# Loading f once and turning the first batch's q and k in two parts, in a fused forgetting-attention and bilinear feed-forward kernel

## The chip, the core and the metric

The kernel runs on one core of one Trainium2 chip. The metric is the device time of one execution in microseconds. A core has a matrix engine (TensorE, PE in the profile), a vector engine (VectorE, DVE), a scalar engine with activation tables (ScalarE, ACT), a general engine (GpSimd, POOL), a sync engine that issues DMAs (SyncE, SP), and 16 DMA engines. Each engine runs its own instructions in the order in which they were written, and waits on semaphores for what other engines produce. PEld in the profile is the loading of weights into TensorE, which overlaps its matmuls.

## The reference

Two stages follow each other. The first is causal attention with a forgetting gate over 8 batches, 8 heads, 576 positions and a head size of 64:

```python
scores = scale * np.matmul(q, k.transpose(0, 1, 3, 2))
log_f = np.log(np.clip(f, 0.0001, 1.0))
cum = np.cumsum(log_f, axis=-1)
decay = cum[:, :, :, None] - cum[:, :, None, :]
scores = np.where(causal, -1000000000.0, scores + decay)
attn = exp(scores - max) / sum
out  = np.matmul(attn, v)
```

The second takes the attention's output as 4608 tokens of 512 numbers and computes `(x @ w_a) * (x @ w_b) @ w_out` with an inner size of 1536. All inputs and the output are float32.

## The kernel before

**Attention.** The work is tiled by t, a pair of heads of one batch (32 tiles), and by u, two tiles that share one set of score matmuls (16 groups of four heads). Within a tile the rows fall into blocks i = 0 to 4 of 128 positions (the last has 64), and only blocks at or below the diagonal are computed. Four score groups g cover the rows: g 0 holds blocks 1 and 0, g 1 block 2, g 2 block 3, g 3 block 4 (`qk_group`, lines 383 to 440).

q and k come in as float32, 128 partitions of 4 heads times 32 slots (`load_qk`, line 280). They are cast to float16 (`cast_qk`, through the helper `cast`, lines 137, 139 and 141) and turned by VectorE's 32x32 transpose (`transpose_qk`, line 294), so that the head's 64 dimensions lie on four row groups of 32 partitions. A score matmul therefore uses 32 rows, and four heads run side by side on the four row groups.

**The decay.** Only the part that depends on the key position matters for a softmax over keys. The cumulated logarithm of f is added to the scores of the first two batches by TensorE: a matmul of a one-hot column (`pick`) with the tile `crow` (line 390, `mm(y, pick, crow)`). `crow` holds, in each of the four row groups of 32 partitions, 16 rows with the high part of the cumulated values in float16 and 16 rows with the low part, so that one matmul adds both. These 16 rows are the heads of batches 0 and 1. For later batches the cumulated values are stored to DRAM (`cum_store`, line 226) and loaded again, spread over all partitions (`load_spread`, line 452), and are added by VectorE.

In the kernel before, f is loaded twice into one tile of 128 partitions: partitions 0 to 63 receive the first 16 rows four times, partitions 64 to 127 all 64 rows (`f_load`, line 194). VectorE clips (line 205), ScalarE takes the logarithm (line 208), VectorE cumulates by a scan (line 212), in two ranges of columns, 0 to 256 and 256 to 576. VectorE then makes `crow` for partitions 0 to 63 from the high part (line 216) and a selector `lsel` (line 219), and a copy puts the same rows into partitions 64 to 127 (line 223).

**Softmax.** For the first two batches (the direct ones) VectorE takes the maximum straight from the scores in PSUM (line 484), ScalarE the exponential with the sum (lines 537, 543), VectorE the reciprocal (lines 550, 552), and GpSimd normalises (line 560). The first batch's probabilities are transposed by TensorE (`pe_tr`, line 584) and copied out of PSUM, those of later batches by DMA (line 576). Products with v (lines 604, 606, 616, 629) are copied into `xT`, which is what the feed-forward stage reads.

**Feed-forward.** For each block of 256 to 512 tokens and each of 12 slices of the inner size, four matmuls give `psa` and four `psb` (line 877). ScalarE or VectorE copies `psa` to float16, VectorE multiplies it with `psb` (line 888), and matmuls with `wout` follow (line 897). The weights come in by GpSimd's DMAs, which also cast them (line 357). The tiles for the second half of the first batch's q and k lie in the memory of `wout` until `wout` is loaded.

**Fillers.** 40 groups of four matmuls on the identity matrix (line 174), whose results nobody uses, stand in TensorE's order at places where it has nothing else to do.

**The order.** All operations are written down first, 2342 of them, each with the engines that may run it. Two tables then fix everything: `ORDER` lists operation numbers in the sequence in which they are issued, and `CHOICE` gives one letter for each operation that has several engines to choose from (A for ScalarE, D for VectorE, P for GpSimd, S for SyncE). No planner runs in the kernel. The feed-forward blocks of early batches are interleaved on TensorE with the attention of later ones.

In the order before, the first operations of SyncE's queue are: f (16 rows four times), k and q of heads 0 to 3, k and q of heads 4 to 7, the first part of v, k and q of the second batch's first half, the last part of v, the store of the cumulated values. ScalarE issues the other load of f. GpSimd's sequence is: paddings (memsets, lines 167 and 169), identity matrix, casts of k and q of heads 0 to 3 in two parts each, the copy of `crow`, a weight load, half of a q cast, a weight load, the other half, a weight load, a cast of v, then normalisations.

Of the kernel before, what the change touches and what calls it, by code (L numbers as in the profile page):

```python
# [37 lines left out]
def kernel(  # L38
# [46 lines left out]
    lsel = fixed("lsel", [128, 1], FP32)  # L85
# [10 lines left out]
    chigh = wout16.rearrange("p n k -> p (n k)")[:, 4608:4608 + S]  # L96
# [60 lines left out]
    def picks(_):  # L157
        nc.vector.tensor_reduce(out=lsel, in_=ident.rearrange("p (a x r) -> p x a r", x=2, r=16)[:, 1],
                                axis=AXXY, op=ADD, negate=True)
# [3 lines left out]
        nc.vector.tensor_scalar(out=neg, in0=eye, scalar1=NEGBIG, scalar2=1.0, op0=MUL, op1=MUL)  # L163

# [20 lines left out]
    def f_tiles():  # L185
        x = [s_pool.tile([128, 1024], FP32, tag="S", name=n) for n in ("cum_f", "cum_l")]
        cw["f"], cw["l"] = x[0][:, 0:S], x[1][:, 0:S]
        cw["1"] = x[0][:, S:].bitcast(FP16)[:, 0:S]

    def f_load(e, m):  # L190
        rows = f.rearrange("b h s -> (b h) s")
        if m == 0:
            rows = bass.AP(rows.tensor, 0, [[0, 4], [S, 16], [1, S]])
        ENG[e].dma_start(out=cw["f"][HP[m]], in_=rows)
# [8 lines left out]
    def clip(lo, hi):  # L203
        x = cw["f"][:, lo:hi]
        nc.vector.tensor_scalar(out=x, in0=x, scalar1=1e-4, scalar2=1.0, op0=MAX, op1=MIN)
# [4 lines left out]
    def scan(lo, hi):  # L210
        x = cw["f"]
        nc.vector.tensor_tensor_scan(out=x[:, lo:hi], data0=cw["1"][:, lo:hi], data1=cw["l"][:, lo:hi],
                                     initial=x[:, lo - 1:lo] if lo else 0.0, op0=MUL, op1=SUB)

    def high_part(lo, hi):
        nc.vector.tensor_copy(out=chigh[HP[0], lo:hi], in_=cw["f"][HP[0], lo:hi])

    def rows_part(lo, hi):
        nc.vector.scalar_tensor_tensor(out=crow[HP[0], lo:hi], in0=chigh[HP[0], lo:hi], scalar=lsel[HP[0]],
                                       in1=cw["f"][HP[0], lo:hi], op0=MUL, op1=ADD)  # L220

    def rows_again(e, lo, hi):
        ENG[e].tensor_copy(out=crow[HP[1], lo:hi], in_=crow[HP[0], lo:hi])

    def cum_store(_):
        nc.sync.dma_start(out=cum_d, in_=cw["f"][HP[1]])

    f_tiles()
    o_f = [op("AS", "ldf", lambda e, m=m: f_load(e, m), size=m) for m in range(2)]
    s_users = [take(o_f[0], "S") for _ in range(2)]  # L230
    o_f[1].after.append(o_f[0])
    o0 = op("D", "ones", f_ones, [])
    o0.after.append(o_f[0])
# [895 lines left out]
```

## Time and profile before

| What | Value |
|---|---|
| Median of the runs shown | 403.06 us (403.03 to 404.61) |
| The profiled execution | 402.69 us |
| Its span | 400.9 us |
| Busy share of PE, DVE, POOL, ACT | 95%, 79%, 66%, 63% |
| Granted TensorE clock, mean | 0.985 of full speed |
| First score matmul starts | 13.34 us |
| First feed-forward matmul starts | 33.89 us |

The span goes from the first to the last record of the program on the core; the time of the execution holds some 1.8 us more around it. A row of the timeline gives the start, the length, the engine and line of one instruction or of a run of like ones (x2, x52), and in brackets the idle time of the engine just before and what ended it. Where a row has no bracket, its engine did not wait. SPq, ACTq and POOLq are the queues of an engine that issue a DMA: the length there is the issuing, not the transfer. The time to landing is given by rows of their own.

### The profile page before, as it was taken

The page shows a single profiled execution, that of the slowest core. Times are in us where ns is not written, and L with a number is a line of the kernel's source. Part 1 is how long each engine was busy: PE and PEld are TensorE (multiplying, and loading weights), DVE is VectorE, ACT ScalarE, POOL GpSimd, SP SyncE. Part 2 cuts the span into 40 slices and gives each one's busy share as a digit, 9 for nine tenths or more (in the row PEclk, how much of TensorE's full clock was granted, in tenths as well). Part 3 has the DMA queues.
Part 4 walks back from the last instruction along what each step waited for, and adds up shares of the span by engine and source line. Part 5 has one row for each costly group of instructions (what it writes and reads, how often), then busy time and mean ns, then how long its engine had stood idle before and what let it go on. Part 6 is the DMA issues. An engine that isn't in the chain of part 4 may idle for free.

```text
span 400.9 us, 10798 instructions
## 1 busy us (share of the span) xinstructions
PE 378.9 (95%) x3856; PEld 209.3 (52%) x3856; DVE 315.5 (79%) x958; ACT 250.6 (63%) x756; POOL 262.8 (66%) x438
## 2 busy tenths in 40 slices
PE   5679799989999999999999999999999999999996
PEld 5557575765846544444545454544454444444553
DVE  5879997979998988989899789899959893373450
ACT  2678895768768777758785777675868673310111
POOL 4988899787967796979696948697858753000000
PEclk9869999999999999999999999999999999999999
DMA  7999999999999999999899998999997827101102
GB/s 245 261 217 224 253 284 224 233 209 225 208 281 224 267 199 305 202 310 191 270 217 286 238 301 168 242 242 243 255 199 192 151 68 177 54 0 53 55 2 78
DMA packets 149466, 80.71 MB, mean 201 GB/s; under 512 B 130660, under 2 KB 133476, under 8 KB 149412
## 3 DMA queue, kind: packets, MB, share of 16 engines
q1 hardware_dynamic: 145492, 75.02, 79.1%
q0 software_dynamic: 3696, 4.72, 7.0%
q8 instruction: 30, 0.49, 0.5%
q10 hardware_dynamic: 224, 0.28, 0.2%
q14 instruction: 24, 0.20, 0.1%
HBM read 52.20 MB, written 9.58 MB: 154 GB/s over the span
## 4 chain that ended last, share of the span: by engine, by line
PE 69%; DMA 8%; DVE 8%; POOL 5%; ACT 4%; issue 4%; SPq 0%; POOLq 0%; ACTq 0%; DVEq 0%
PE psb L877 20%; PE psa L877 20%; PE pso L897 16%; PE sc L390 7%; DVE st L484 3%; PE pv L604 2%; DMA PTB<-PB 2%; POOL PA L560 2%; DMA spread<-cum_d 2%; DMA k<-in_k_dram 2%; PE idle L174 1%; DVE ht L888 1%; DVE S L508 1%; DMA out_dram<-osb 1%; DMA xT<-PA 1%
## 5 line engine op out<-in xcount | busy, mean ns | idle before, releaser
L877 PE MATMUL psb<-xT,wb 128*128 128x512 f16 (+2 forms) x528 | 115.2, 341 | 2.4 <-DVE a L141 1.3
L877 PE MATMUL psa<-xT,wa 128*128 128x512 f16 (+2 forms) x528 | 115.2, 341 | 0.5 <-ACT osb L137 0.2
L508 DVE CUSTOM_DVE_ANT_0 S<-sc,spread 128x128 f32<-128x128 f32 (+3 forms) x192 | 104.3, 567 | 7.8 <-PE sc L390 6.7
L560 POOL TENSOR_SCALAR PA<-PA,st 128x128 f16<-128x128 f16 (+2 forms) x180 | 84.4, 482 | 33.8 <-DVE st L552 19.8
L897 PE MATMUL pso<-wout,ht 128*128 128x512 f16 (+1 forms) x444 | 98.4, 374 | 0.0
L888 DVE TENSOR_TENSOR ht<-psb,a 128x512 f16<-128x512 f32 (+2 forms) x132 | 76.7, 588 | 14.1 <-PE psb L877 10.1
L543 ACT ACTIVATE PA<-S,st 128x256 f16<-128x256 f32 (+2 forms) x144 | 71.9, 501 | 22.9 <-DVE st L508 21.4
L877 PEld LDWEIGHTS <-wb 128*128 128x128 f16 x528 | 49.8, 98 | 45.7 <-issue 6.8
L877 PEld LDWEIGHTS <-wa 128*128 128x128 f16 x528 | 50.4, 98 | 42.7 <-issue 2.0
L560 POOL TENSOR_SCALAR PB<-PB,st 128x512 f16<-128x512 f16 (+1 forms) x90 | 62.8, 712 | 10.6 <-DVE st L552 5.9
L897 PEld LDWEIGHTS <-ht 128*128 128x128 f16 x444 | 41.8, 98 | 48.1 <-issue 2.8
L137 ACT CAST a<-psa 128x512 f16<-128x512 f32 (+2 forms) x85 | 42.7, 511 | 34.8 <-PE psa L877 33.4
L390 PE MATMUL sc<-kT,qT 32*128 32x128 f16 (+5 forms) x960 | 41.3, 272 | 6.8 <-DVE qT L294 4.6
L543 ACT ACTIVATE PB<-S,st 128x512 f16<-128x512 f32 x48 | 34.3, 716 | 8.1 <-DVE st L508 7.4
L484 DVE TENSOR_REDUCE st<-sc 128x1 f32<-128x576 f32 (+8 forms) x48 | 31.4, 693 | 6.8 <-PE sc L390 5.2
L141 DVE CAST a<-psa 128x512 f16<-128x512 f32 (+2 forms) x47 | 26.2, 558 | 11.3 <-PE psa L877 10.8
L390 PEld LDWEIGHTS <-qT 32*128 32x128 f16 (+1 forms) x960 | 19.0, 96 | 28.8 <-issue 12.3
L552 DVE RECIPROCAL st<-st 128x2 f32<-128x2 f32 x128 | 18.6, 157 | 11.5 <-ACT PB L543 6.1
L537 ACT ACTIVATE PB<-S,st 128x576 f16<-128x576 f32 x24 | 18.6, 775 | 13.9 <-DVE st L508 5.0
L543 ACT ACTIVATION_READ_ACCUMULATOR PA<-S,st 128x1 f32 x144 | 27.2, 189 | 0.0
L137 ACT COPY osb<-pso 128x512 f32<-128x512 f32 (+1 forms) x26 | 14.4, 563 | 20.3 <-PE pso L897 18.6
L141 POOL CAST k<-k 128x1152 f16<-128x1152 f32 (+2 forms) x16 | 22.1, 1384 | 5.0 <-DMA k<-in_k_dram 5.0
(87 smaller groups left out, 449.8 us busy)
## 6 DMA issues: line engine op xcount, KB each, us to landing
spread<-cum_d SPq DMA_DIRECT2D x24, 576.0 KB, 5.9
out_dram<-osb SPq DMA_DIRECT2D x35, 256.0 KB, 4.0
k<-in_k_dram SPq DMA_DIRECT2D x15, 576.0 KB, 6.5
q<-in_q_dram SPq DMA_DIRECT2D x15, 576.0 KB, 6.9
v<-in_v_dram SPq DMA_DIRECT2D x32, 256.0 KB, 6.7
wout<-in_moe_w_out_dram POOLq DMA_DIRECT2D x3, 512.0 KB, 11.0
wa<-in_moe_w_a_dram POOLq DMA_DIRECT2D x1, 1024.0 KB, 13.9
v<-in_v_dram SPq DMA_DIRECT2D x8, 128.0 KB, 6.0
```

Of the source, the lines that this page charges most:

```text
L137: nc.scalar.copy(out=out_, in_=in_)
L141: ENG[e].tensor_copy(out=out_, in_=in_)
L390: nc.tensor.matmul(out=dst, lhsT=lhsT, rhs=rhs, start=start, stop=stop, skip_group_check=True)
L484: nc.vector.tensor_reduce(out=m if i == 4 else st[:, 2 * i:2 * i + 2][:, h:h + 1] if isinstance(x, list) else m, in_=y, axis=AXX, op=MAX, ...
L508: nc.vector.tensor_tensor_reduce(out=o, in0=x, in1=y, scale=-1.0, scalar=3e38, op0=ADD, op1=MIN, accum_out=m)
L537: nc.scalar.activation(out=p_blocks(t, 4), in_=T[("s" if direct else "z", t, 4)], func=EXP, bias=st[:, 8:9], scale=sign, accum_out=st[:, 1 ...
L543: nc.scalar.activation(out=p_blocks(t, i)[:, :, h, :], in_=x.rearrange("p (j k) -> p j k", k=128), func=EXP, scale=sign, bias=st[:, c:c + ...
L552: nc.vector.reciprocal(out=st[:, 20 + 2 * i:22 + 2 * i], in_=st[:, 10 + 2 * i:12 + 2 * i])
L560: ENG[e].tensor_scalar(out=p, in0=p, scalar1=st[:, c:c + 1], scalar2=1.0, op0=MUL, op1=MUL)
L877: nc.tensor.matmul(out=p[:, 0:n], lhsT=w16[:, db, 128 * fb:128 * fb + 128], rhs=xTflat[db][:, t0:t0 + n], start=(db == 0), stop=(db == 3))
L888: nc.vector.tensor_tensor(out=ht[:, 0:n], in0=T.pop(("psb", t0, fb))[:, 0:n], in1=T.pop(("a16", t0, fb))[:, 0:n], op=MUL)
L897: nc.tensor.matmul(out=o, lhsT=T[("ht", t0, fb)][:, 128 * tb:128 * tb + 128], rhs=wout16[:, fb, c], start=(fb == 0), stop=(fb == 11))
```

## The change

The program now has 2351 operations. Four things differ.

1. **f.** All 64 rows are loaded once, into partitions 0 to 63, by one DMA; clip, logarithm and scan work on 64 partitions. From the first 32 partitions a high part in float16 and a low part (the value less the high part) are put into a scratch tile `parts`. TensorE then spreads them: two accumulating matmuls with a matrix of zeros and ones, `sel`, put the high part into the first 16 and the low part into the second 16 rows of all four row groups, and one copy out of PSUM makes `crow`. `sel` is made on VectorE with a memset and two copies; `lsel` and the copy between partition halves go.
2. **q and k of the first batch** are loaded, cast and turned in two parts: tokens 0 to 255 and tokens 256 to 575. The first scores of a group (g 0, blocks 0 and 1) depend on the first parts alone; before, they depended on the whole. Casts were in two parts before, split at 5 of 9, and are now split at 4 of 9; a transpose now depends only on the cast of its part. Each part's load may be issued by SyncE or ScalarE.
3. **New numbers and a new order.** `ORDER` and `CHOICE` are replaced.
4. A small function `turns` names which parts TensorE transposes; they are the same ones as before.

```diff
-    chigh = wout16.rearrange("p n k -> p (n k)")[:, 4608:4608 + S]
+    sel = spare[2][0:32, 1536:1792].rearrange("p (e m) -> p e m", e=2)
+    parts = wout16.rearrange("p n k -> p (n k)")[0:32, 4608:4608 + 2 * S].rearrange("p (e s) -> p e s", e=2)
...
+        nc.vector.memset(sel, 0.0)
+        for e in range(2):
+            nc.vector.tensor_copy(out=sel[:, e].rearrange("p (g e r) -> p g e r", e=2, r=16)[:, :, e],
+                                  in_=eye[0:32, 0:16].unsqueeze(1).to_broadcast([32, 4, 16]))
...
-    def f_load(e, m):
-        rows = f.rearrange("b h s -> (b h) s")
-        if m == 0:
-            rows = bass.AP(rows.tensor, 0, [[0, 4], [S, 16], [1, S]])
-        ENG[e].dma_start(out=cw["f"][HP[m]], in_=rows)
+    def f_load(e):
+        ENG[e].dma_start(out=cw["f"], in_=f.rearrange("b h s -> (b h) s"))
...
-    def rows_part(lo, hi):
-        nc.vector.scalar_tensor_tensor(out=crow[HP[0], lo:hi], in0=chigh[HP[0], lo:hi], scalar=lsel[HP[0]],
-                                       in1=cw["f"][HP[0], lo:hi], op0=MUL, op1=ADD)
-
-    def rows_again(e, lo, hi):
-        ENG[e].tensor_copy(out=crow[HP[1], lo:hi], in_=crow[HP[0], lo:hi])
+    def high_part(e, lo, hi):
+        cast(e, parts[:, 0, lo:hi], cw["f"][0:32, lo:hi])
+
+    def low_part(e, lo, hi):
+        ENG[e].tensor_tensor(out=parts[:, 1, lo:hi], in0=cw["f"][0:32, lo:hi], in1=parts[:, 0, lo:hi], op=SUB)
+
+    def rows_mm(lo, hi):
+        c = T[("rows", lo)] = ps.tile([128, 512], FP32, tag="ff", bufs=RING["ff"], name="rows")
+        for e in range(2):
+            nc.tensor.matmul(out=c[:, 0:hi - lo], lhsT=sel[:, e], rhs=parts[:, e, lo:hi], start=e == 0, stop=e == 1)
+
+    def rows_ev(e, lo, hi):
+        cast(e, crow[:, lo:hi], T.pop(("rows", lo))[:, 0:hi - lo])
...
+    SPLIT = [(0, 4), (4, TW)]
...
+    def load_part(e, which, hh, m):
...
+        lo, hi = SPLIT[m]
+        src = src_of[which][0, 4 * hh:4 * hh + 4, 64 * lo:64 * hi, :].rearrange("h (s t) d -> h s (t d)", s=NSLOT)
+        ENG[e].dma_start(out=T[key][:, 128 * lo:128 * hi], in_=src)
...
-    def transpose_qk(b, which, hh):
+    def transpose_qk(b, which, hh, lo=0, hi=TW):
...
-                deps = [T_ops[(x, 0, u)] for x in "qk"] + [o_low, o_pick] + crow_ops[:1 if g == 0 else 2]
+                deps = [y for x in "qk" for y in T_ops[(x, 0, u)][:1 if g == 0 else 2]] + [o_low, o_pick] + crow_ops[:1 if g == 0 else 2]
```

The two tables are too long to show. Decoded, the new sequences begin as follows (q00 is the first part of q of heads 0 to 3, q01 its second part, q10 and q11 the parts of heads 4 to 7, and so for k):

| Engine | New sequence at the start |
|---|---|
| SP, loads | f, k00, q01, k01, q10, v blocks 0 and 1, k11, q of batch 1, store of the cumulated values, v of batch 1, k of batch 1 |
| ACT | load q00, logarithm's table, both logarithms, loads q11 and k10, cast q01, cast k01, `crow` first range out of PSUM, exponential's table, cast k10, three exponentials of the first tile, `crow` second range, exponentials |
| POOL | identity matrix, cast k00, cast q00, load of wa from column 512 on, load of wb up to column 512, casts q10 and q11, paddings, cast of v, twelve normalisations, load of wa up to column 512 |
| DVE | selectors, ones, masks, both clips, scan, high and low part of the first range, turn k00, scan of the second range, turn q00, q01, k01, maxima of the first tile, high and low part of the second range, a maximum of the second tile, turn k10 and q10, a maximum and two reciprocals, cast k11, maxima of the second pair |
| PE | 14 fillers, spreading of the first range, filler, scores g 0 of heads 0 to 3, 5 fillers, spreading of the second range, 5 fillers, scores g 0 of heads 4 to 7 |

After the first batch the new sequence on TensorE sets each score group behind nearly the same number of feed-forward matmuls as the old one.

185 lines of the change are left out of this document (97 added, 88 removed), and 133 rows, old and new, of the table ORDER.

## The prediction

> **What bounds the kernel now.** I read the windows first, then the timeline of the first 34 us, then the landing times of the DMAs issued there. The profiled execution took 402.69 us, 1.8 more than its span:
>
> ```profile
> span 400.9 us, 10798 instructions
> ```
>
> The columns of the next two fences are the stretch, its length, the busy time of PE, PEld, DVE, ACT, POOL (the second: PE and PEld of the filler matmuls of line 174 alone), the granted clock, the DMA share and GB/s.
>
> ```profile
> 0.00:4.00 4.00, 1.13 (x11) 1.14 (x12) 1.72 (x7) 1.49 (x2) 2.09 (x12) 1.00 0.39 78
> 4.00:8.00 4.00, 4.00 (x51) 4.00 (x49) 1.61 (x9) 0.78 (x2) 0.17 (x1) 1.00 1.00 327
> ...
> 0.00:34.00 34.00, 22.72 (x370) 19.55 (x370) 25.12 (x63) 20.23 (x65) 25.78 (x50) 0.85 0.98 237
> 34.00:57.00 23.00, 20.32 (x383) 15.98 (x382) 21.46 (x51) 19.84 (x56) 19.45 (x29) 1.00 1.09 249
> 80.00:320.00 240.00, 236.98 (x2292) 120.00 (x2293) 211.42 (x723) 173.64 (x534) 188.09 (x314) 1.00 1.03 235
> 320.00:380.00 60.00, 60.00 (x400) 28.94 (x397) 31.22 (x68) 17.73 (x42) 9.33 (x17) 1.00 0.25 68
> ```
>
> ```profile
> 0.00:34.00 34.00, 12.92 (x144) 11.67 (x144) 0.85 0.98 237
> ```
>
> From 80 us on PE is never without work: 3.0 us idle in 240, none in the 60 after that, where the other engines are mostly idle and PE drains feed-forward matmuls that have long been ready. So the end is set by the amount of PE work plus what PE loses early. Up to 34 us PE is busy 22.72 us, 12.92 of it fillers, so 9.8 us of real work in 34 us. A microsecond gained ahead of the first feed-forward matmul is a microsecond off the end, as long as nothing behind it slips. Read the other way: the chain there is worth 24 us, and the rest of the kernel has little to give.
>
> The timeline of that stretch (start, duration, engine, line, operation, and the idle time before with its releaser):
>
> ```profile
> 0.73 0.56 ACTq L194 DMA_DIRECT2D cum_f<-in_f_dram  x1
> 0.74 0.75 SPq L194 DMA_DIRECT2D cum_f<-in_f_dram  x1
> 1.19 0.99 POOL L169 MEMSET nv<- 64x512 f16 x2
> 1.55 0.54 SPq L280 DMA_DIRECT2D k<-in_k_dram  x1
> 4.11 3.85 SPq L264 DMA_DIRECT2D v<-in_v_dram  x2
> 6.78 0.53 DVE L205 TENSOR_SCALAR cum_f<-cum_f 128x256 f32<-128x256 f32 x2 [2.03 <-DMA cum_f<-in_f_dram]
> 7.11 0.78 ACT L208 ACTIVATE cum_l<-cum_f 128x256 f32<-128x256 f32 x2 [4.28 <-DVE cum_f L205]
> 7.83 2.52 POOL L141 CAST k<-k 128x640 f16<-128x640 f32 x2 [5.02 <-DMA k<-in_k_dram]
> 8.28 0.76 DVE L216 CAST wout<-cum_f 64x256 f16<-64x256 f32 x1
> 10.34 1.55 POOL L139 TENSOR_SCALAR q<-q 128x640 f16<-128x640 f32 x2
> 11.64 1.50 ACT L137 CAST k<-wout 128x640 f16<-128x640 f32 x2 [3.75 <-DVE kT L294]
> 12.09 1.19 DVE L294 STREAM_TRANSPOSE qT<-q 128x576 f32<-128x576 f32 x1
> 12.87 0.94 POOL L357 DMA_DIRECT2D wa<-in_moe_w_a_dram  x1 [0.16 <-issue]
> 13.16 1.28 ACT L201 ACT_TABLE_LOAD   x1
> 13.34 0.40 PE L390 MATMUL sc<-kT,qT 32*128 32x256 f16 x8 [4.64 <-DVE qT L294]
> 14.40 4.32 PE L174 MATMUL idle<-ident 128*128 128x128 f16 x52
> 14.51 1.29 DVE L484 TENSOR_REDUCE st<-sc 128x2 f32<-128x512 f32 x2
> 15.24 0.47 ACT L543 ACTIVATE PA<-sc,st 128x256 f16<-128x256 f32 x1 [0.58 <-DVE st L484]
> 17.00 1.05 POOL L141 CAST nv<-v 128x1024 f16<-128x1024 f32 x1
> 18.08 0.69 SPq L264 DMA_DIRECT2D v<-in_v_dram  x1
> 18.32 2.30 POOL L560 TENSOR_SCALAR PA<-PA,st 128x128 f16<-128x128 f16 x5 [0.27 <-DVE st L552]
> 18.65 0.50 PE L390 MATMUL sc<-kT,qT 32*128 32x256 f16 x8
> 20.36 0.47 ACT L543 ACTIVATE spread<-sc,st 128x256 f16<-128x256 f32 x1 [0.94 <-DVE st L484]
> 33.89 0.60 PE L877 MATMUL psa<-xT,wa 128*128 128x256 f16 x4
> ```
>
> The first scores start at 13.34 because q's transpose ends then, behind two whole casts on POOL, behind a k that is usable at 7.83. The cumulated f is no gate here. The second pair of head groups starts its scores at 18.65, the exponentials of that pair at 20.36, the first feed-forward matmul at 33.89.
>
> **The change, part by part.** Its order, decoded from operation numbers, puts each group of scores after the same amount of feed-forward work as before: never more than 1.9 us of matmuls apart (count of columns at the pace of this trace), equal for most groups after the third batch. So I take the middle and the tail at no change, with that as the bound, and work out the start alone.
>
> *Loads.* A part of k or q is 4/9 (262 KB) or 5/9 (328 KB) of 590 KB. The order of need is f (147 KB), q's first part on ACT's queue, k's first part, q's second, k's second on SP's. Delivered so far: 4 x 78 = 312 KB by 4 us, then 327 KB a microsecond. Whole k of before stands behind two f loads, 885 KB in all, which this pace passes at 5.75; its cast starts at 7.83, 2.1 later, and I take that offset for every part. First k part: 671 KB, 5.1, usable at 7.2. Second q part: 999 KB, 8.2. Second k part: 1327 KB, 9.2.
>
> ```profile
> cum_f<-in_f_dram ACTq DMA_DIRECT2D x1, 144.0 KB, 2.7
> wout<-in_q_dram SPq DMA_DIRECT2D x1, 576.0 KB, 9.0
> wa<-in_moe_w_a_dram POOLq DMA_DIRECT2D x1, 1024.0 KB, 13.9
> wa<-in_moe_w_a_dram POOLq DMA_DIRECT2D x1, 512.0 KB, 8.5
> wb<-in_moe_w_b_dram POOLq DMA_DIRECT2D x1, 512.0 KB, 9.7
> v<-in_v_dram SPq DMA_DIRECT2D x1, 128.0 KB, 11.4
> ```
>
> These rows give KB and us from issue to landing. *f* is now loaded once. It lands between 3.4 (issue 0.73 plus 2.7, as on ACT's queue) and 6.78 (as now). Even at 6.78, scan, high part, low part and the spreading matmuls follow within 3 us (the high part's cast was 0.76 at its worst), before 9.9, so this part by itself is worth nothing: it lies under the k and q loads. What it removes, half a DMA of descriptors and the copies between partition halves, hides there too.
>
> *Casts and transposes.* POOL casts the first parts: k 7.2 to 8.4 (half of 2.52, a little less for 512 columns), q to 9.2 (half of 1.55). DVE turns them, half of 1.19 each, to 9.8. ACT casts the second parts, 0.75 each: q 8.2 to 9.0, k 9.2 to 10.0, and only then evicts the spread f rows (not in this trace; the nearest row is the 0.47 of the exponential, which reads as many columns from PSUM; half and twice that are the bounds, I take 0.4). First scores: 10.4 against 13.34, 2.9 earlier. The two second-part transposes (0.66 each) end at 11.1 on DVE, the maxima start 1.2 after the scores as now: 11.6 against 14.51. ACT loads the exponential's table from 10.4 to 11.9 (1.28 and a warming call), casts the first part of the second k (0.73), and starts the exponentials at 12.6 against 15.24: 2.6 earlier.
>
> *POOL's queue.* The paddings (nv's 0.99 and four smaller memsets, 1.5 in all by the first row's start and the identity matrix behind them) move from ahead of the identity matrix to ahead of v's cast. The identity comes 1.5 sooner, which only starts fillers sooner. Behind the first q cast at 9.2 POOL has two weight issues (0.94 each), both casts of the second q (1.55) and the paddings: v's cast from 14.2 to 15.3, then twelve normalisations at 2.30/5, to 20.8. Before, the normalisations started at 18.32.
>
> *Second pair.* Behind the maxima of the first tile DVE has the f tail's high and low part and the next maxima (about 2.5 together), then two half transposes: 15.3, so its scores at 15.3 against 18.65. The ten fillers between the two groups of scores (40 matmuls at 4.32/52) take 3.3 from about 11.5, so they end about then too. DVE then casts the last k part (0.75, as on ACT) ahead of the maxima of the second pair; exponentials at 17.5 against 20.36: 2.8 earlier. That part, issued behind v at 8.0, lands 2.7 to 9.0 later, 10.7 to 17.0; DVE comes to it at about 16, so the late end would cost 1.0. I take it as landed by then, and keep the 1.0 for the range.
>
> *Sum.* The three gates move by 2.6 to 3.4, and I carry 2.8, less 0.2 for four spreading matmuls, two more casts and four more issues, to the first feed-forward matmul: about 31.3. 402.69 - 2.6 = 400.1 for a profiled execution; the median shown lies 0.37 above that execution, hence 400.4. The unknown costs: filling the selector and the low part's subtraction on DVE, each between nothing and the 0.76 of line 216. The first lies under the 2.03 that DVE waited for f, the subtraction for the first columns under the load of k, and both are taken at nothing; with that cover gone up to 1.5 would come onto the sum. The cast of the last k part on DVE, which was not there, is 0.75 and is on the path; it is counted.
>
> A rule on the first part of the second k, ACT's last load. Here ACT's f landed in 2.7 while SP's f, issued with it, held the clip until 6.78. The Trainium skill, "DMA: Bandwidth & Descriptors", section "Queues, rings and completion order", says that each DMA engine takes packets in turn from every queue that has work, so a short queue need not wait for a long one; the two f rows agree. By that rule this part lands early and the sum stays 400.4; by the rows of SP's queue alone it would be that of the first rival.
>
> **Rivals.** *Hidden anyway.* ACT's last k part is issued behind both logarithms (now ending 7.89) and two issues of 0.56, so by 9.0 at the latest. It lands 2.7 (ACT's empty queue) to 9.0 (fifth on SP's) later, 11.7 to 18. ACT's cast of it stands ahead of every exponential, so from a landing at 14.5 on nothing is left of the gain. The last k part on SP holds DVE's maxima in the same way from 18.5 on. For it: the queues are full from 4 us on. Against: ACT's queue has been the quick one. Price: the gain falls to 0 to 1; 402.6.
>
> *Slower: the weights.* POOL now issues 1.5 MB of weights right after the first q cast, from 9.2 instead of 12.87, and issues the 512 KB of wa that the first feed-forward matmul needs only behind twelve normalisations, which stand behind the cast of v. A v issued into the weights landed in 11.4. v's second DMA is issued by 7.96 and would land at 19.4, be cast by 20.4, the normalisations (2.30/5 each) end at 25.9, and wa land 10.7 later (mean of 8.5, 9.7 and 13.9) at 36.6, 2.7 after 33.89: 405.4, on the median 405.8. It decides once v lands after 16.7. Against: v is issued before the weights now, and its cast at 17.00 waited for no DMA. In the forecast v is in by 14.2, the normalisations end at 20.8, and wa, now last of the weights, lands in the 8.5 of its own row, at 29.3, 2.0 before it is needed.
>
> *More than that.* If earlier batch-1 inputs also close the 2.7 us of idle between 34 and 57, 400.4 - 2.7 = 397.7. Against: DVE is 93% busy there.
>
> **How the numbers follow.** Forecast 0.52 (its own range 399.0 to 401.8), hidden 0.24, slower 0.13, more 0.11. What a measurement can tell from 403.06 is about 0.5%, so 401.05 and 405.07 are the bounds: faster 0.59 (most of the forecast and all of "more"), same 0.28, slower 0.13. Range 397.9 to 404.8, which leaves out most of the slower case and the lower half of "more", 0.15 to 0.2 in all.
>
> **What would show it.** First scores near 10.4, with ACT's eviction of the f rows as the last thing they wait for; exponentials near 12.6 and 17.5; first psa near 31.3, the 80 to 320 stretch as busy as now. It is wrong if psa waits for the DMA of wa, if ACT or DVE idles for a k part after 13 us, or if PE idles more than 3.0 us between 80 and 320.

## The result, and the profile after

The changed kernel is slower. Its median is 425.89 us (425.33 to 428.38) against 403.65 us (403.03 to 404.61) of the kernel before on the same chip, a ratio of 1.056 (95% interval 1.051 to 1.061), some 22 us more. The forecast was 400.4, the upper end of the range 404.8. The profiled execution took 426.45 us.

The page of the changed kernel, its span and two of the rows of 40 slices (tenths of busy time; a slice is 10.6 us):

```profile
span 424.7 us, 10828 instructions
...
PE   5042789997899999999999999999999999999996
...
DMA  2937789989999999999999999999988927300102
```

TensorE is almost idle in the second slice and at two tenths in the fourth, and the DMA engines are at 0.2 and 0.3 in the first and the third (the weights, which GpSimd issues at 10.6 and 11.6, fill the second). The stretch from 4 to 10 us, in which the first q and k travel, after and then before (columns as in the prediction, the last two being DMA share and GB/s):

```profile
4.00:10.00 6.00, 3.03 (x39) 2.54 (x37) 1.95 (x6) 0.78 (x2) 0.72 (x2) 1.00 0.26 102
```

```profile
4.00:10.00 6.00, 4.70 (x60) 4.52 (x57) 3.42 (x11) 0.78 (x2) 2.17 (x2) 1.00 1.01 355
```

Loads were issued and waiting all the time, and yet the 16 DMA engines were busy for 0.26 of it, against 1.01 before, and moved 102 GB/s instead of 355. A quarter of the engines at work would look like this. The timeline of the changed kernel shows what waited for it:

```profile
4.06 0.52 DVE L204 TENSOR_SCALAR cum_f<-cum_f 64x256 f32<-64x256 f32 x2
4.43 21.83 SPq L269 DMA_DIRECT2D v<-in_v_dram  x2
9.28 0.71 POOL L141 CAST k<-k 128x512 f16<-128x512 f32 x1 [7.97 <-DMA k<-in_k_dram]
11.95 0.40 PE L412 MATMUL sc<-kT,qT 32*128 32x256 f16 x4 [4.92 <-DVE qT L308]
13.11 0.87 ACT L135 ACTIVATE q<-q 128x640 f16<-128x640 f32 x1 [7.96 <-DMA q<-in_q_dram]
19.91 0.86 ACT L137 CAST k<-k 128x640 f16<-128x640 f32 x1 [5.93 <-DMA k<-in_k_dram]
21.61 0.40 PE L412 MATMUL sc<-kT,qT 32*128 32x256 f16 x4 [9.26 <-DVE kT L308]
...
29.92 1.54 POOL L139 TENSOR_SCALAR q<-wout 128x512 f16<-128x512 f32 x2 [17.59 <-DMA wout<-in_q_dram]
...
54.87 0.60 PE L902 MATMUL psa<-xT,wa 128*128 128x256 f16 x4
```

f comes early (clip at 4.06 instead of 6.78), but the first k part is cast at 9.28, the second parts of q and k at 13.11 and 19.91, the second q at 29.92, and SyncE is held for 21.83 us in the issue of v. The first feed-forward matmul starts at 54.87 instead of 33.89, 21.0 us later; the end follows with 22. The eight parts together hold 2 x 2 x (256 + 320) KB = 2304 KB, 2.36 MB, which at 102 GB/s alone would take 23 us.

One sentence of "The change" does not hold on the chip: that the first scores of a group depend on the first parts alone. Only their first four matmuls, over the first half of the head size, do so (11.95, behind the first transpose of q). The others wait until 21.61 for the second transpose of k, which follows the cast at 19.91. So the second parts set the first scores here too. The second transpose writes columns of the same tile on both sides of those that these other matmuls read; that they wait for this reason fits the code, but no run tests it.

Three stretches of the changed kernel:

```profile
0.00:34.00 34.00, 11.31 (x144) 9.61 (x144) 10.71 (x31) 7.18 (x14) 6.62 (x18) 0.72 0.54 128
34.00:57.00 23.00, 14.73 (x234) 10.72 (x238) 15.89 (x41) 16.71 (x61) 16.23 (x28) 0.67 0.76 186
...
80.00:320.00 240.00, 233.72 (x2377) 122.45 (x2376) 207.62 (x693) 173.51 (x535) 188.80 (x310) 1.00 1.08 236
```

No engine is busy for more than a third of the first 34 us, and TensorE runs at a granted clock of 0.72 and 0.67 up to 57 us, where it had 0.85 and 1.00 before. From 80 us on the matmuls stand nearly as close as before (6.3 us idle in 240, against 3.0).

### The profile page after: what moved, and what is told of

Same layout as the page of the kernel before. It is cut to its first block, busy times and chain, and to the rows that moved or that the text cites. A ratio compares the mean times of both kernels' runs of the same rounds, so it can differ in the third digit from the quotient of the medians.

```text
span 424.7 us, 10828 instructions
## 1 busy us (share of the span) xinstructions
PE 381.6 (90%) x3860; PEld 209.8 (49%) x3860; DVE 313.1 (74%) x960; ACT 255.8 (60%) x764; POOL 258.7 (61%) x434
## 3 DMA queue, kind: packets, MB, share of 16 engines
HBM read 52.05 MB, written 9.58 MB: 145 GB/s over the span
## 4 chain that ended last, share of the span: by engine, by line
PE 64%; DMA 11%; POOL 7%; SPq 6%; DVE 5%; issue 3%; ACT 3%; POOLq 0%; ACTq 0%; DVEq 0%
PE pso L922 19%; PE psb L902 17%; PE psa L902 16%; PE sc L412 6%; SPq L269 5%; DMA wout<-in_k_dram 3%; POOL PB L582 3%; DMA spread<-cum_d 2%; DMA PTB<-PB 2%; POOL PA L582 2%; DVE st L506 2%; DMA xT<-PA 2%; PE pv L626 2%; DVE ht L913 1%; ACT spread L565 1%
## 5 line engine op out<-in xcount | busy, mean ns | idle before, releaser
L582 POOL TENSOR_SCALAR PA<-PA,st 128x256 f16<-128x256 f16 (+2 forms) x180 | 83.8, 480 | 38.2 <-DVE st L574 27.0
L913 DVE TENSOR_TENSOR ht<-psb,a 128x512 f16<-128x512 f32 (+2 forms) x132 | 76.3, 587 | 19.6 <-PE psb L902 16.1
L565 ACT ACTIVATE PA<-S,st 128x256 f16<-128x256 f32 (+2 forms) x144 | 72.0, 502 | 21.8 <-DVE st L530 19.6
L137 ACT CAST a<-psa 128x512 f16<-128x512 f32 (+2 forms) x92 | 46.7, 511 | 37.5 <-PE psa L902 29.5
L308 DVE STREAM_TRANSPOSE kT<-k 128x576 f32<-128x576 f32 (+2 forms) x18 | 19.7, 1097 | 18.0 <-ACT k L137 14.2
L137 ACT COPY osb<-pso 128x512 f32<-128x512 f32 (+1 forms) x26 | 14.5, 566 | 25.1 <-PE pso L922 23.5
L480 POOL TENSOR_SCALAR_AFFINE_SELECT spread<-spread 128x768 f32<-128x768 f32 x24 | 20.8, 868 | 13.2 <-DMA spread<-cum_d 13.2
L574 DVE RECIPROCAL st<-st 128x2 f32<-128x2 f32 x128 | 18.8, 157 | 12.6 <-ACT PA L565 8.4
L141 DVE CAST a<-psa 128x512 f16<-128x512 f32 (+2 forms) x40 | 22.6, 564 | 6.7 <-PE psa L902 6.3
L137 ACT CAST xT<-pv 128x512 f16<-128x512 f32 (+2 forms) x37 | 16.7, 456 | 17.8 <-PE pv L628 11.5
```

The source lines that it names most:

```text
L137: nc.scalar.copy(out=out_, in_=in_)
L141: ENG[e].tensor_copy(out=out_, in_=in_)
L480: nc.gpsimd.affine_select(out=c[:, :, 0:SM].rearrange("p h (j k) -> p h j k", k=128), in_=c[:, :, SM:2 * SM].rearrange("p h (j k) -> p h j ...
L565: nc.scalar.activation(out=p_blocks(t, i)[:, :, h, :], in_=x.rearrange("p (j k) -> p j k", k=128), func=EXP, scale=sign, bias=st[:, c:c + ...
L582: ENG[e].tensor_scalar(out=p, in0=p, scalar1=st[:, c:c + 1], scalar2=1.0, op0=MUL, op1=MUL)
L913: nc.vector.tensor_tensor(out=ht[:, 0:n], in0=T.pop(("psb", t0, fb))[:, 0:n], in1=T.pop(("a16", t0, fb))[:, 0:n], op=MUL)
```

## The experiments

All ratios are to the kernel before on the same chip, with the 95% interval; "us" beside them is the ratio's distance from 1 times that kernel's median there (404.5 to 405.4).

**contig16: parts that are contiguous.** This kernel reads other tokens than the change does. What differs between a whole load and a part is the shape of its source. The whole load's heads and slots merge into one dimension of 128; a part is a slice of each head, so its slowest dimension is the 4 heads.

```diff
-        src = src_of[which][0, 4 * hh:4 * hh + 4, 64 * lo:64 * hi, :].rearrange("h (s t) d -> h s (t d)", s=NSLOT)
+        x = src_of[which][0, 4 * hh:4 * hh + 4].rearrange("h s d -> (h s d)")
+        src = x[0:128 * 128 * (hi - lo)].rearrange("(p x) -> p x", p=128)
```

> The changed kernel, with the eight part loads reading one contiguous stretch of the same number of bytes instead of their tokens (so q and k of the first batch hold other tokens; the work on them is the same). Same number of DMAs, same bytes to each partition, same order. Theory A (a part load, whose source is four heads by 32 slots, moves on four of the 16 DMA engines; the changed kernel shows a DMA share of 0.26 at 102 GB/s from 4 to 10 us, 4/16 = 0.25): all part loads are usable by 13 us, DMA share near 1 from 4 us on, first feed-forward matmul near 31 us, time 397 to 404, as my prediction's steps have it. Theory B (more and smaller DMAs, or v's long issue of 21.8 us in SP's queue, hold the loads): nothing changes, time 420 to 427.

Measured: 404.72 us, ratio 0.9998 (0.9963 to 1.0033). The 21 us are gone. Its stretch from 4 to 10 us and its timeline:

```profile
4.00:10.00 6.00, 3.19 (x43) 2.29 (x41) 5.36 (x11) 4.23 (x7) 3.45 (x4) 1.00 1.05 291
```

```profile
5.03 0.71 POOL L141 CAST k<-k 128x512 f16<-128x512 f32 x1 [3.73 <-DMA k<-in_k_dram]
...
5.37 0.44 ACTq L295 DMA_DIRECT2D wout<-in_k_dram  x1
10.64 0.29 PE L413 MATMUL sc<-kT,qT 32*128 32x256 f16 x4 [1.14 <-DVE kT L309]
12.24 0.73 ACT L137 CAST k<-wout 128x512 f16<-128x512 f32 x1 [2.39 <-DMA wout<-in_k_dram]
12.88 0.47 ACT L566 ACTIVATE PA<-sc,st 128x256 f16<-128x256 f32 x1
15.56 0.50 PE L413 MATMUL sc<-kT,qT 32*128 32x256 f16 x8
17.27 0.47 ACT L566 ACTIVATE spread<-sc,st 128x256 f16<-128x256 f32 x1 [0.21 <-DVE st L507]
31.42 0.61 PE L903 MATMUL psa<-xT,wa 128*128 128x256 f16 x4 [0.38 <-DMA wa<-in_moe_w_a_dram]
```

With the same bytes in the same number of DMAs, the share is back at 1.05. And the start now comes as forecast: first full scores 10.64 (10.4), exponentials 12.88 (12.6), second pair 15.56 and 17.27 (15.3 and 17.5), first feed-forward matmul 31.42 (31.3). Yet the end does not move: of the 2.5 us at the first feed-forward matmul nothing is left there. That is a second question, taken up below. (The six other kernels with this start and this order up to there, all described below, had their first feed-forward matmul at 31.87 to 32.79, so 31.42 is the early end of what this start gives.)

**before_four: the old kernel with such a source.** The rows of a head start 17 tokens apart instead of 18, so that heads and slots no longer merge; other tokens are read, in the same amount and by the same number of DMAs.

```diff
+        if b == 0:
+            src = bass.AP(src.tensor, 4 * hh * S * D, [[S * D, 4], [17 * D, NSLOT], [1, 18 * D]])
```

> The kernel before, with one thing changed: the four whole loads of the first batch's q and k read four heads by 32 slots with a slot step of 17 tokens instead of 18, so that the two dimensions no longer merge into one of 128 (other tokens are read; bytes and number of DMAs are the same). Theory A: these 2.36 MB move at about 100 GB/s instead of 355 from 4 to 10 us, the fourth load lands near 26 us instead of 12, and the time rises by 12 to 22 us, to 415 to 425. Theory B: the number and size of DMAs is as before, so the time stays at 403 to 405.

Measured: 423.81 us, ratio 1.048 (1.043 to 1.054), 19.6 us more with nothing else of the change. Windows and timeline:

```profile
4.00:10.00 6.00, 5.21 (x60) 5.04 (x57) 2.95 (x11) 0.78 (x2) 0.00 (x0) 1.00 0.26 90
```

```profile
12.98 1.51 POOL L141 CAST k<-k 128x640 f16<-128x640 f32 x2 [10.17 <-DMA k<-in_k_dram]
22.21 0.61 PE L392 MATMUL sc<-kT,qT 32*128 32x256 f16 x8 [13.00 <-DVE qT L296]
53.06 0.60 PE L879 MATMUL psa<-xT,wa 128*128 128x256 f16 x4
```

The same 0.26, and the same late start. So a source of this shape makes a loss of nearly this size by itself, and with whole loads as with parts. The Trainium skill, "DMA: Bandwidth & Descriptors", section "Why a DMA increments its semaphore by 16 and not by 1", says that the number of engines is the largest one up to 16 that divides the slowest dimension of both sides of the transfer. With 4 heads on the source side that is 4 of 16, and the share of 0.26 agrees.

**perhead16: each part as four DMAs of one head.** This computes all that the change computes.

```diff
-        ENG[e].dma_start(out=T[key][:, 128 * lo:128 * hi], in_=src)
+        for h in range(4):
+            src = src_of[which][0, 4 * hh + h, 64 * lo:64 * hi, :].rearrange("(s t) d -> s (t d)", s=NSLOT)
+            ENG[e].dma_start(out=T[key][RG[h], 128 * lo:128 * hi], in_=src)
```

> The changed kernel, with each of the eight part loads issued as four DMAs, one head and 32 partitions each, so that the outermost dimension of the source is 32 slots and not four heads. Complete computation. Theory A: DMA share near 1, all loads usable by 15 us; the 24 added issues at about 0.5 us each cost some of it, above all on ScalarE, where eight of them stand ahead of its casts (about 4 us); time 399 to 408. Theory B (many small DMAs are the cause): four times as many, so the time goes up, over 426.

Measured: 414.63 us, ratio 1.025 (1.022 to 1.029). Its stretch from 4 to 10 us:

```profile
4.00:10.00 6.00, 4.53 (x43) 3.63 (x41) 4.02 (x9) 2.15 (x4) 3.48 (x4) 1.00 0.69 176
```

```profile
13.74 2.50 ACTq L295 DMA_DIRECT2D wout<-in_k_dram  x4
18.75 0.40 PE L413 MATMUL sc<-kT,qT 32*128 32x256 f16 x4 [8.88 <-DVE kT L309]
```

Half of the loss is gone, less than expected. The first parts are early (the first four score matmuls start at 9.58), but 32 issues instead of 8 stand on the two queues, and the engines are busy for only 0.69. ScalarE's eight issues last until 16.24; its casts of the second parts of q and k stand behind them, at 16.28 and 17.06, so the full first scores come at 18.75 and the first feed-forward matmul at 41.14.

**before_f16, before_f16act: f's repeated load in the kernel before.** That load has a slowest dimension of 4 too, the four repetitions. Here it is four DMAs of 16 rows each, on SyncE's queue or on ScalarE's.

```diff
         if m == 0:
-            rows = bass.AP(rows.tensor, 0, [[0, 4], [S, 16], [1, S]])
+            for g in range(4):
+                ENG[e].dma_start(out=cw["f"][16 * g:16 * g + 16], in_=rows[0:16])
+            return
```

(before_f16act has `nc.scalar` in the place of `ENG[e]`.)

> The kernel before, with one thing changed: SP's load of f, 16 rows repeated four times with an outermost dimension of four, is issued as four DMAs of 16 rows. Complete computation. Theory A: f lands near 4.5 us instead of 6.78, so the clip starts 1.5 to 2.3 us sooner. By my prediction f is no gate, so the time stays within 1 us of before, 402 to 404.5, unless the three further issues on SP, ahead of k, push k back by 1.5 us: then up to 405. Rival: f gates the first scores after all, and the time falls by 1 to 2 us.

> The kernel before, with f's repeated rows loaded by four DMAs of 16 rows, as in before_f16, but issued by ScalarE, so that k and q are the first DMAs of SP. Complete computation. Theory: in before_f16 k was issued at 2.57 and its cast started at 6.87; now k is issued at 0.74 and cast from 5.0 to 5.8, the first scores come near 10.3 instead of 11.66 and the time is 0.5 to 1.5 us under before_f16, 0.990 to 0.994 of before. Rival D (what is gained ahead of 57 us is waited for again between 57 and 80): no better than before_f16, 0.994 to 1.0.

Measured: before_f16 402.25 us, ratio 0.994 (0.992 to 0.997), 2.3 us less; before_f16act 405.78, ratio 1.006 (1.002 to 1.009). The timelines of the one and of the other:

```profile
4.77 0.53 DVE L207 TENSOR_SCALAR cum_f<-cum_f 128x256 f32<-128x256 f32 x2
6.87 1.80 POOL L141 CAST k<-k 128x640 f16<-128x640 f32 x2 [4.06 <-DMA k<-in_k_dram]
11.66 0.40 PE L392 MATMUL sc<-kT,qT 32*128 32x256 f16 x8 [3.46 <-DVE qT L296]
32.26 0.60 PE L879 MATMUL psa<-xT,wa 128*128 128x256 f16 x4
```

```profile
4.90 1.51 POOL L141 CAST k<-k 128x640 f16<-128x640 f32 x2 [2.09 <-DMA k<-in_k_dram]
10.02 0.53 DVE L207 TENSOR_SCALAR cum_f<-cum_f 128x256 f32<-128x256 f32 x2 [5.27 <-DMA cum_f<-in_f_dram]
15.12 0.61 PE L392 MATMUL sc<-kT,qT 32*128 32x256 f16 x8 [5.70 <-DVE qT L296]
```

With f in four DMAs of 16 rows it is clipped at 4.77 instead of 6.78, k cast at 6.87 instead of 7.83, and the first feed-forward matmul comes 1.6 us earlier; the end comes 2.3 us earlier. So f did stand in the way, as the rival had it. This version computes all that the kernel before computes and is 0.6% faster than it. On ScalarE's queue the whole k goes first and is cast at 4.90, but five loads of f one behind the other there are clipped only at 10.02, VectorE then has f's steps in front of both transposes, and the scores are later than before; the gain that was expected of this run did not come.

**before_fonce, before_fonce_act: the f part of the change alone.** The order before, with f loaded once and spread by TensorE; VectorE copies the rows out of PSUM. In before_fonce_act the low part and the spreading of the first columns stand ahead of the second scan, and ScalarE copies.

```diff
+            ENG[e].dma_start(out=cw["f"], in_=rows)
...
+        for x in range(2):
+            nc.tensor.matmul(out=c[:, 0:hi - lo], lhsT=sel[:, x], rhs=parts[:, x, lo:hi], start=x == 0, stop=x == 1)
+        nc.vector.tensor_copy(out=crow[:, lo:hi], in_=c[:, 0:hi - lo])
```

```diff
-        nc.vector.tensor_copy(out=crow[:, lo:hi], in_=c[:, 0:hi - lo])
+        cast("D" if lo else "A", crow[:, lo:hi], c[:, 0:hi - lo])
...
+        early_ops = [ops[n] for n in (50, 51)]
+        seq = [o for o in seq if o not in early_ops]
+        at = seq.index(ops[49]) + 1
+        seq[at:at] = early_ops
```

> The kernel before with the f part of the change alone, in the old order: f loaded once by SP, high and low part, two spreading matmuls and a copy out of PSUM by VectorE (there is one engine fewer in the copy than before, GpSimd). q and k are loaded whole. Complete computation. My prediction: f by itself is worth nothing, 0.998 to 1.002. What before_f16 showed: f's load with an outermost dimension of four held the clip until 6.78 and pushed SP's queue back; without it the clip starts near 4.6, k's cast near 6.2, and the time falls by 1.5 to 3 us, 0.992 to 0.997.

> before_fonce (the order before, f loaded once and spread by TensorE), with the low part of the first 256 columns and their spreading moved ahead of the second scan on VectorE, and the copy out of PSUM on ScalarE ahead of its casts. In before_fonce these VectorE steps (0.71 and 0.42 us) and the wait between them stood ahead of q's transpose, which could have started when q's cast ended, at 10.05, and started at 11.11. Theory: transpose of q at 10.1, first scores near 11.5 instead of 12.91, end some 1.4 us below before_fonce: ratio about 0.994 to the kernel before. Rival: k's transpose is late by the 0.7 that now stands ahead of it and nothing is gained: 0.998.

Measured: before_fonce 403.47 us, ratio 0.998 (0.995 to 1.000); before_fonce_act 405.13, ratio 1.002 (0.999 to 1.006). Both miss what was expected of them. The f part is worth about a microsecond (0.998 of 405.1), by the interval 0 to 2. In before_fonce the wait of VectorE for f is gone, and its transpose of q is late instead; moving f's steps ahead made k's transpose late, as the rival had it, behind a second scan of 1.34:

```profile
11.11 1.20 DVE L297 STREAM_TRANSPOSE qT<-q 128x576 f32<-128x576 f32 x1
12.91 0.61 PE L393 MATMUL sc<-kT,qT 32*128 32x256 f16 x8
```

```profile
9.13 1.34 DVE L213 TENSOR_TENSOR_SCAN cum_f<-cum_f,cum_l 64x320 f32<-64x320 f16 x1 [1.23 <-ACT cum_l L209]
10.40 1.18 DVE L297 STREAM_TRANSPOSE kT<-k 128x576 f32<-128x576 f32 x1
13.92 0.40 PE L393 MATMUL sc<-kT,qT 32*128 32x256 f16 x8
```

**contig16_whole: the new order with whole loads.** Each tensor half in one DMA again, on 16 engines; casts and transposes stay in parts.

```diff
+        if m == 0:
+            src = src_of[which][0, 4 * hh:4 * hh + 4].rearrange("h (s t) d -> (h s) (t d)", s=NSLOT)
+            ENG[e].dma_start(out=T[key], in_=src)
```

> The changed kernel and its order, but each of the four q and k tensors of the first batch loaded by one merged DMA of 590 KB where its first part was loaded, and no load for the second part (the partitions hold other tokens; the work on them is the same). It keeps casts and transposes in two parts, and undoes only the loading in parts. Theory: 16 engines, but the first part now waits for the whole: k usable near 6 us, the second q and k of the first pair at the same time as the first parts, so the first scores come at 9.5 to 11.5 us, about as in contig16 (10.64), because there the last second part is what they wait for too; time within 0.4% of contig16. Rival: loading in parts is what brings the first scores forward; then first scores after 12 us and the time 1 to 2 us above contig16.

Measured: 406.22 us, ratio 1.005 (1.002 to 1.007), half a per cent above contig16, as the rival had it.

```profile
13.01 0.40 PE L412 MATMUL sc<-kT,qT 32*128 32x256 f16 x4 [1.02 <-DVE kT L308]
34.05 0.60 PE L902 MATMUL psa<-xT,wa 128*128 128x256 f16 x4
```

The full first scores start at 13.01 against 10.64. Loading in parts, if all engines carry it, is worth 1.3 to 2.6 us at the first feed-forward matmul (34.05 against 31.42 to 32.79). And this kernel starts its first feed-forward matmul within 0.5 us of before_fonce (34.51), with the new order in the place of the old, and ends 2.8 us behind it, which points to a cost of the new order behind the start.

**contig16_pvlater: TensorE's longest wait taken away.** In contig16 TensorE waits 2.73 us at 72 us for a transposing DMA. Four operations, two of them TensorE's that wait and two copies behind them, are moved some way back.

```diff
+        late_ops = [ops[n] for n in (361, 357, 362, 358)]
+        seq = [o for o in seq if o not in late_ops]
+        at = seq.index(ops[1717]) + 1
+        seq[at:at] = late_ops
```

> The kernel contig16 (the changed kernel with its part loads reading contiguous bytes, other tokens, same work), with one thing changed: in TensorE's order the two products with v of tile 4 that waited 2.73 us at 71.9 for a DMA transpose, and their copies, stand behind five and a half more groups of feed-forward matmuls that needed nothing. Theory C (the 2.5 us by which contig16 reaches its first feed-forward matmul sooner are lost at this one wait and in the half clock of the 4 us behind it): the wait is gone, the granted clock from 70 to 80 is 1.00 instead of 0.83, the time falls by 2 to 4 us, to 0.990 to 0.996 of before. Rival D (the stretch from 57 to 80 is bound by GpSimd's normalisations and the DMA transposes, so that TensorE only waits at the next place): the time stays within 0.4% of before.

Measured: 404.13 us, ratio 1.000 (0.997 to 1.003). A row of its timeline:

```profile
76.67 0.36 PE L639 MATMUL pv<-xT,nv 128*64 128x128 f16 x6 [1.20 <-DVE ht L914]
```

The wait for that DMA is gone, but TensorE waits at the next places instead, and its granted clock is 0.95 from 70 to 80 us and 0.50 from 80 to 82. So the wait is a sign of the loss, not its place.

**rest_old_31, 45, 60, 75, 200: where the new order loses.** contig16 with the new order for the first 185, 295, 390, 560 or 1150 operations, which is up to about the time in the name; all operations behind stand in the order, and on the engines, of the kernel before. Only the two tables are edited, here where the first cut lies:

```diff
         242 168 270 243 7 19 222 271
-        1638 277 1639 1642 281 278 89 1640 173 1641 287 223 180 162 96 202
...
+        26 3 38 2 29 36 32 13 277 92 162 223 236 1638 1639 173
...
```

 Of the 2166 behind the first cut, 108 stand on another engine in the changed kernel.

> contig16 (the changed kernel with its part loads made contiguous, so other tokens of the same arrays), but only the first 185 operations keep the new order, up to the first feed-forward matmul; all that follow stand in the order and on the engines of the kernel before. Theory A, the new order of the rest gives back the start's gain: first feed-forward matmul at 31 to 32 us, and the end moves with it, 2 to 3 us below the kernel before (ratio 0.993 to 0.995). Theory B, a microsecond at the first feed-forward matmul isn't a microsecond at the end in this start, whatever follows: ratio 1.000, as contig16. If A is right by half, 0.997.

> as rest_old_31, but the new order is kept for 295 operations, to about 45 us. Loss between 31 and 45 us: ratio 1.000 or above. Loss behind 45 us: 0.993. Both halves share it: 0.997.

> as rest_old_31, but the new order is kept for 390 operations, to about 60 us, with the place at which GpSimd waited 2.3 us for the cumulated values of a third-batch tile, but not the 170 operations behind it. If that wait, or what leads to it, is the loss: ratio 1.000 or above. If the loss needs the order of 60 to 75 us: 0.993.

> as rest_old_31, but the new order is kept for 560 operations, up to about the 50th feed-forward operation, near 75 us; the rest as before. Theory A with the loss between 31 and 75 us (the wait of 2.7 us at 72 us and the lower clock behind it): ratio 1.000. Theory A with the loss behind 75 us: ratio 0.993 to 0.995, as rest_old_31. Theory B: 1.000 for both.

> as rest_old_31, but the new order is kept for 1150 operations, near 200 us. Loss behind 200 us: ratio 0.993 to 0.995. Loss ahead of 200 us, or theory B: 1.000.

| New order up to | Ratio (interval) | us |
|---|---|---|
| 31 us | 0.993 (0.990 to 0.997) | -2.7 |
| 45 us | 0.993 (0.990 to 0.995) | -3.0 |
| 60 us | 1.007 (1.004 to 1.009) | +2.7 |
| 75 us | 1.004 (1.002 to 1.007) | +1.7 |
| 200 us | 1.000 (0.996 to 1.003) | -0.2 |
| the end (contig16) | 1.000 (0.996 to 1.003) | 0 |

When the old order follows, the new start is worth 2.7 to 3.0 us at the end. The first feed-forward matmul is no measure of it, though, as the first cut (31 us) and the second (45 us) show:

```profile
35.08 0.60 PE L903 MATMUL psa<-xT,wa 128*128 128x256 f16 x4
```

```profile
32.79 0.38 PE L903 MATMUL psa<-xT,wa 128*128 128x256 f16 x2
```

With the first cut that matmul was expected at 31 to 32 us, and it starts 1.2 us later than in the kernel before. Nor can the traces show where the 3 us come off: the profiled executions of the two and of the kernel before last 402.91, 402.56 and 402.69 us, and the gain is one of medians. The step from the cut at 45 us to the one at 60 us points to the loss standing in what the new order does between them. It does not prove it: the cuts at 60 and 75 us are even worse than the whole new order, so a seam between two orders seems to have a price of its own, and that price can hide what the rest does.

**contig16_mask_later: one operation moved.** In that stretch of contig16 GpSimd waits once for long. The operation masks the cumulated values of tile 9 (`mask_copy`), and its load (`load_spread`) stands only 3 operations ahead of it in the new order, 125 in the old one.

```diff
+        seq.remove(ops[473])
+        seq.insert(seq.index(ops[451]) + 1, ops[473])
```

> contig16 with one operation moved: GpSimd's masking of the cumulated values of tile 9 (the one that waited 2.32 us for its DMA at 61.14 us) stands behind three normalisations and the cast of k that followed it. If that wait is where the start's gain goes: the normalisations come up to 3.2 us earlier, TensorE's wait of 2.7 us at 72 us shrinks by as much, ratio 0.993. If it is covered, as TensorE's wait was: 1.000, as contig16.

Measured: 402.87 us, ratio 0.996 (0.993 to 0.998), 1.8 us less, where 0.993 was expected. Timeline of contig16, then of this kernel:

```profile
51.67 0.38 SPq L475 DMA_DIRECT2D spread<-cum_d  x1
61.14 0.87 POOL L481 TENSOR_SCALAR_AFFINE_SELECT spread<-spread 128x768 f32<-128x768 f32 x1 [2.32 <-DMA spread<-cum_d]
74.63 0.35 PE L652 MATMUL pv<-PTB,nv 128*64 128x64 f16 x10 [2.73 <-DMA PTB<-PB]
...
77.24 1.06 PE L903 MATMUL psb<-xT,wb 128*128 128x256 f16 x4
```

```profile
52.82 0.38 SPq L475 DMA_DIRECT2D spread<-cum_d  x1
63.32 0.87 POOL L481 TENSOR_SCALAR_AFFINE_SELECT spread<-spread 128x768 f32<-128x768 f32 x1
72.42 0.35 PE L652 MATMUL pv<-PTB,nv 128*64 128x64 f16 x10
```

Masked later, the operation finds its data there, the normalisations that were queued behind it come earlier, and the product with v that had waited 2.73 us starts at 72.42 without a wait, though this execution was 1.2 us late at its first feed-forward matmul (32.58). The stretch from 70 to 80 us in contig16 and here:

```profile
70.00:80.00 10.00, 7.27 (x86) 5.27 (x84) 5.56 (x13) 4.74 (x16) 9.81 (x17) 0.83 1.35 206
```

```profile
70.00:80.00 10.00, 9.70 (x166) 7.43 (x163) 9.12 (x22) 7.86 (x25) 10.00 (x18) 1.00 1.07 185
```

So by the medians this one wait of GpSimd, whose normalisations the other engines need, took 1.8 of the 2.7 to 3.0 us. Against the kernel before the gain is clear; against contig16 alone (0.996 to 1.003) it is at the edge of the noise. Three kernels that keep a wait at this place (2.3 us in contig16, 1.5 in contig16_pvlater, 1.6 in rest_old_200) all gave 1.000. What takes the remaining microsecond stays open; the interval of this run reaches 0.993, at which nothing would remain, and 0.998, at which two thirds would.

## Why the prediction was wrong, point by point

*Loads* is the step that failed, and it carries all of the 22 us. It priced a part by its bytes, at the 327 KB a microsecond of the stretch in which whole loads moved, and so assumed that a part moves as a whole load does. The prediction put the first k part, the second q part and the second k part at 7.2, 8.2 and 9.2 us; they were cast at 9.28, 13.11 and 19.91. The term was not mis-sized by a little: the pace belonged to another shape of transfer. The diff showed it (the part's pattern keeps the heads apart, `h s (t d)`, where the whole one merges them, `(h s) (t d)`), and a row that the prediction quoted was its trace in the kernel before: f's repeated load on SyncE's queue, with a slowest dimension of 4, issued at 0.74, let the clip start only at 6.78, where ScalarE's whole one took 2.7 to land. The prediction read that difference as one of queues. before_f16 shows that it was one of shape.

*Casts, transposes, second pair* came out right in their times, and partly by luck. contig16, which has the change's order without the slow loads, meets the gates within 0.3 us. But there the parts were some 2 us sooner than forecast (first k part cast at 5.03, not 7.2; second parts of q and k at 6.37 and 7.19, not 8.2 and 9.2), and the gates were not, because something else held each of them. The first full scores waited for the second transpose of k, which ends at 10.58, and not for ScalarE's eviction of the f rows, done at 8.33. The first exponential waited for a k part until 12.24. The first feed-forward matmul waited for wa, which landed 9.4 us after its issue at 21.95, so that nothing was left of the 2.0 us that it was to be early. One sum does not come out as worded either: 15.3 for the second pair adds 2.5 and 1.2 to 11.6, at which the first tile's maxima begin, and not to their end, 1.29 later.

*f by itself worth nothing* was nearly right for the change's own f part (before_fonce, a ratio of 0.998), and wrong in its reason. The prediction had the f load hide under k and q; it stood in front of them, and in another shape it brings k earlier by 1 us (before_f16).

*The middle at no change* failed too, and would have cost the forecast its gain even with good loads: contig16 has an early first feed-forward matmul and nothing of it at the end. The comparison of the two orders behind it counted TensorE's matmuls ahead of each group of scores, and did not look at GpSimd's and SyncE's orders, where a load and its user had moved to within 3 operations of each other. That a microsecond gained ahead of the first feed-forward matmul is one off the end is not borne out: before_f16 fits it (1.6 us there, 2.3 at the end), but rest_old_31 ends 2.7 us earlier with that matmul 1.2 us later, and rest_old_60 2.7 us later with it 1.6 us earlier (32.33).

*The rivals.* "Slower: the weights" had the sign, not the mechanism. The row of the first feed-forward matmul after has no wait for wa, and contig16 has one of 0.38 us. "Hidden anyway" saw that a late last k part holds ScalarE, but for its queue: in contig16 that part, issued at 5.37 behind the others on ScalarE's queue, was in at 12.24, 6.9 later. That lies between the 2.7 and 9.0 that the prediction had for it, and ahead of the 14.5 from which it would have hurt. That a transfer's own shape would slow it was not among the rivals. Of the signs set out beforehand two came true: ScalarE idled 5.93 us for a k part until 19.91, and TensorE idled 240 - 233.72 = 6.3 us between 80 and 320 us.

## What to carry to other kernels

Before a load is split, write down the slowest dimension of both its sides: a slice that no longer merges with the dimension above it can leave a transfer of the same bytes on a quarter of the engines, and a DMA share of 0.26 while loads wait is the sign to look for. A pace read from one shape of transfer is no price for another. After a split, see in the trace whether the first user really waits for the first part alone. When a new order is compared with an old one, look at every queue, and at the distance between a load and the operation that waits for it on an engine on which others depend.

## What the runs showed of the hardware that was not expected

While loads of q and k with a slowest dimension of 4 were under way (4 to 10 us), the core's DMA moved 90 to 102 GB/s at a share of 0.26; with 128 it was 291 to 355 GB/s at 1.01 to 1.05. f's load with four repetitions (a step of 0) was slow too: f was clipped at 6.78, and at 4.77 when four DMAs of 16 rows took its place. Its own rate was not measured.

Behind such transfers even the issue of the next ones is long: SyncE's two issues of v took 21.83 us after, 3.85 before and 1.24 in contig16.

After a wait of TensorE of 2.73 us in contig16, four matmuls of 128x256 took 1.06 us in place of 0.61, from 76.4 to 79 us, at a granted clock of 0.50 from 76 to 78. rest_old_200 (2.68 us) and contig16_whole (2.65 us) show the same drop behind such a wait. It is no rule: in rest_old_75 a wait of 2.56 us was followed by none, with 1.00 up to 90 us, and in before_f16 the clock was 0.50 from 72 to 74 us behind a wait of only 1.40. What decides stays open.
